# Attention and gated feed-forward on one core: the first slots' transposes, loads and copies put in another order

## The chip, the core and the metric

The kernel runs on one core of one Trainium2 chip. Its time is the device time of one execution in microseconds. Eleven runs gave a median of 563.99 us, the lowest 562.91 us and the highest 565.9 us. A run of the changed kernel is compared with runs of this one on the same chip.

## What is computed

Threshold attention over 8 batches of 8 heads, 576 positions, head size 64, then a two-layer block with a gated activation on the 4608 x 512 result:

```
scores = q @ k.T / sqrt(64)
scores = where(scores >= max(scores, row) - tau, scores, -1e9)
attn = softmax(scores)            # tau = 0.02
x = (attn @ v), heads side by side: 4608 x 512
h = x @ w_in                      # 512 -> 2048
g = h * clip(h + 3, 0, 6) / 6
out = g @ w_out                   # 2048 -> 512
```

Inputs and output are float32. The weights, the values and the normalised attention are kept on the chip in bf16, queries, keys and scores in float32.

## The kernel before

The 64 heads are taken in 16 quads of four heads. A quad is two pairs (pair 0 and pair 1 of the quad), and is worked off in nine **slots**: slots 0 to 3 are the four 128-row blocks of the first pair, 4 to 7 those of the second pair, and slot 8 holds the last 64 rows of all four heads. The 144 slots are numbered by n (the loop at L439); n = 9 x quad + slot. The order of the work on each engine is written out by hand: what the Python loop emits first stands first in its engine's queue, and each engine works in that order.

One turn of the loop does this, in order:
- ScalarE: the exponentials of the slot before (`sm_exp`, L291, two of 128 x 576).
- VectorE: the row maxima of this slot's scores, which also copy them out of PSUM (`sm_max`, L278, two), and on GpSimd the biases made from them (L281, two tiny ones).
- TensorE, from n = 23 on: a piece of the first layer (`mm1`, L354), its relu on ScalarE or VectorE (L363, L365) and its gate on VectorE (L371). All these use the one PSUM tile "h".
- TensorE: if slot n - 2 is marked `on_chip`, nine transposes of its normalised attention into the same tile "h" (L315), and a VectorE copy of them (L316). Slots not so marked are transposed by a DMA on SyncE's queue (L307). `on_chip` holds for odd n below N1 = 22.
- VectorE: the reciprocals of the row sums of slot n - 1 (L294). Then pieces of the second layer (`mm2_part`, L383).
- ScalarE: the masks of this slot (`sm_mask`, L286, two), which wait for the biases.
- TensorE: a transpose step for keys and queries (below), or the products of attention and values (`av_main`, `av_rest`, L324 and L327); then **the scores of the next slot** (L257 or L263), which need the next slot's queries and keys transposed and a free one of two score tiles.
- GpSimd: the normalisation of slot n - 1 (`sm_norm`, L299, two of 128 x 576), and SyncE's DMA transpose of it.
- The issue of loads: `start(loads, ...)` on SyncE's queue for q and k (L515), `start(vcasts, ...)` and `start(casts, ...)` on GpSimd's queue for v and the weights, which are cast to bf16 on the way (L516, L517). A GpSimd DMA stands in GpSimd's queue behind the normalisation and ahead of the next slot's biases.

The transpose step: the second pair's queries in slot 1 and keys in slot 2 of its own quad; the next quad's first pair in slots 5 and 6, and the rest rows of that quad in slot 7 (`transpose_rest`, L229). For the first two batches (quads 0 to 3) queries go through TensorE too. Each writes a PSUM bank, and is followed by copies to SBUF. Key copies go through `copy_out` (L200): VectorE while 0 <= n < 22, ScalarE before the loop and from n = 22 on. Query copies are always VectorE's. `transpose_rest` fills one bank with the keys' and the queries' rest and reads it with two key copies, and then one query copy.

Ahead of the loop: the q and k loads of quad 0 are issued in five steps (L154: first pair's keys, first pair's queries, the rest rows, second pair's keys, second pair's queries). TensorE transposes what the first slots need; GpSimd then makes a one-column copy of the transposed keys into a tile `gate` that nobody reads (L426), and issues the four loads of v behind it (L427). Weights come as 32 loads, 16 of w_in and then 16 of w_out. At L515 to L517 two q/k loads are started in each of the first three slots and then one, no v loads in the first 13 slots, and two weight loads in each of the first four and then one.

Of the kernel before, what the change touches and what calls it, by code (L numbers as in the profile page):

```python
# [9 lines left out]
F32 = mybir.dt.float32  # L10
# [5 lines left out]
P = 128  # L16
# [5 lines left out]
def kernel(  # L22
# [10 lines left out]
    nc = tc.nc  # L33
    B, H, S, D = q.shape
# [8 lines left out]
    N1 = 22  # L43
# [4 lines left out]
    singles = ctx.enter_context(tc.tile_pool(name="singles", bufs=1))  # L48
# [25 lines left out]
    loads = []  # L74
    casts = []
    vcasts = []
# [3 lines left out]
    def load_quad(quad):  # L80
        b, g = divmod(quad, 2)
        nat[quad] = (nat_pool.tile([P, 1152], F32, tag="nq", name="nq"),
                     nat_pool.tile([P, 4, 4, D], F32, tag="km", name="km"),
                     nat_pool.tile([P, 2 * D], F32, tag="kr", name="kr"))
        nq, km, kr = nat[quad]

        def main(dst, src, h, order):
            nc.sync.dma_start(out=dst[:, :, h, :], in_=src[b, 4 * g + h, 0:512, :].rearrange(order, t=4))

        def blocks_q(n, a, j):  # L90
            c = 32 * (2 * a + j)
            nc.sync.dma_start(out=nq[c:c + 32, n * S:(n + 1) * S].rearrange("p (k d) -> p k d", d=32),  # L92
                              in_=q[b, 4 * g + 2 * n + a, :, 32 * j:32 * j + 32].rearrange("(k r) d -> r k d", r=32))

        def load_q(n):
            if b < NB:
                for a in range(2):
                    main(nq[:, 0:1024].rearrange("p (t h d) -> p t h d", h=4, t=4), q, 2 * n + a, "(t p) d -> p t d")
            else:
                for a in range(2):  # L100
                    for j in range(2):
                        blocks_q(n, a, j)

        def rest():
            for dst, src in ((kr[:], k), (nq[:, 1024:1152], q))[0:2 if b < NB else 1]:
                for n in range(2):
                    nc.sync.dma_start(out=dst[64 * n:64 * n + 64, :].rearrange("p (h d) -> p h d", h=2),
                                      in_=src[b, 4 * g + 2 * n:4 * g + 2 * n + 2, 512:S, :].rearrange("h p d -> p h d"))

        for n in range(2):  # L110
            loads.append(lambda n=n: [main(km, k, 2 * n + a, "(p t) d -> p t d") for a in range(2)])
            loads.append(lambda n=n: load_q(n))
            if n == 0:
                loads.append(rest)
# [34 lines left out]
    def start(jobs, n):  # L149
        for _ in range(min(n, len(jobs))):  # L150
            jobs.pop(0)()
# [27 lines left out]
    def alloc_qk(quad):  # L179
        qkT[quad] = (qk_pool.tile([P, 2, S], F32, tag="qT", name="qT"),  # L180
                     qk_pool.tile([P, 2, S + 64], F32, tag="kT", name="kT"))
# [4 lines left out]
    def kT_of(pair):  # L186
        return qkT[pair // 2][1][:, pair % 2, :]
# [4 lines left out]
    def bank(name):  # L192
        nonlocal turn
        turn += 1
        if now < N2 and turn % 2:
            return ps_o.tile([P, 512], F32, tag="o", name=name)
        return ps_m.tile([P, 512], F32, tag="m", name=name)


    def copy_out(out, in_):  # L200
        if 0 <= now < N1:
            nc.vector.tensor_copy(out=out, in_=in_)
        else:
            nc.scalar.copy(out=out, in_=in_)  # L204


    def by_pe(pair):
        return pair // NPAIR < NB
# [16 lines left out]
    def transpose_k(pair):  # L225
        ps = main_pe(nat[pair // 2][1], pair)
        return lambda: copy_out(kT_of(pair)[:, 64:576], ps[:])

    def transpose_rest(quad):  # L229
        ps = bank("tr")  # L230
        nq, _, kr = nat[quad]
        nc.tensor.transpose(ps[:, 0:P], kr[:], identf[:])
        if by_pe(2 * quad):
            nc.tensor.transpose(ps[:, P:2 * P], nq[:, 1024:1152], identf[:])

        def evict():
            qT, kT = qkT[quad]
            both = ps[:].rearrange("p (w n t) -> p w n t", n=2, t=64)
            copy_out(kT[0:64, :, S:S + 64], both[0:64, 0])
            copy_out(kT[64:P, :, 0:64], both[64:P, 0])  # L240
            if by_pe(2 * quad):
                nc.vector.tensor_copy(out=qT[:, :, 512:S], in_=both[:, 1])
        return evict

    def keys(pair, a, hf):
# [43 lines left out]
    def sm_exp(sl, i):  # L289
        s = sl.s[:, i, :]  # L290
        nc.scalar.activation(out=s, in_=s, func=Act.Exp, accum_out=sl.rsum[:, i:i + 1])  # L291

    def sm_recip(sl):
        nc.vector.reciprocal(out=sl.rinv[:], in_=sl.rsum[:])  # L294
# [73 lines left out]
    def mm1_gate(item, hps, r):  # L368
        b, ni, c0, w = item
        c0 += (b % 2) * S  # L370
        nc.vector.scalar_tensor_tensor(out=gbuf[:, ni:ni + 2, c0:c0 + w], in0=r, scalar=6.0, in1=hps,  # L371
                                       op0=Alu.min, op1=Alu.mult)
# [42 lines left out]
        return items  # L415

    alloc_qk(0)
    gate = singles.tile([P, 1], F32)
    evict = transpose_k(0)
    warm_up(4)  # L420
    evict_q = transpose_q(0)
# [1 line left out]
    evict_q()  # L423
    transpose_rest(0)()

    nc.gpsimd.tensor_copy(out=gate[:], in_=kT_of(0)[:, 64:65])  # L426
    start(vcasts, 4)  # L427

    queue = []
    for quad in range(NQUAD):  # L430
        for slot in range(NSLOT):
            sl = Slot()
            sl.quad, sl.slot = quad, slot
            sl.on_chip = len(queue) < N1 and len(queue) % 2 == 1
            queue.append(sl)
    queue[0].tiles = scores(0, 0)

# [1 line left out]
    for n, sl in enumerate(queue):  # L439
        quad, slot = sl.quad, sl.slot  # L440
        b, g = divmod(quad, 2)
        now = n
        if slot in (0, 4):
            pts[2 * quad + slot // 4] = pt_pool.tile([P, 9, 512], BF16, tag="pT", name="pT")
        if slot == 8:
            ptr[quad] = ptr_pool.tile([P, 9, P], BF16, tag="pR", name="pR")
        if quad == 0 and slot == 0:
            load_quad(1)
        if slot == (4 if quad else 8) and quad + 2 < NQUAD:
            load_quad(quad + 2)  # L450
        if slot == 0 and g == 1 and b + 1 < B:
            load_v(b + 1)
        if prev is not None:
            for i in range(2):
                sm_exp(prev, i)
        sm_max(sl)

        if slot != 8 and todo1:
            item, then = todo1.pop(0)
            h = mm1(item)  # L460
            r = mm1_relu(h, on_act=(slot in (0, 1, 3, 5)))
            mm1_gate(item, h, r)
            todo2.extend(then)
        copies = pe_transpose(queue[n - 2]) if n > 1 and queue[n - 2].on_chip else None
        if prev is not None:
            sm_recip(prev)
        if copies:
            copies()
        outs = []


        pieces = 0 if slot == 3 else 1
        if slot == 0:
            second = True
        if second and slot < 2 and len(todo2) > 1 and todo2[0][1] == todo2[1][1]:
            pieces, second = 2, False
        for _ in range(pieces):
            if todo2:
                bb, mt, part = todo2.pop(0)
                mm2_part(bb, mt, part)  # L480
                if part == 3:
                    outs += mm2_out(bb, mt, on_act=False)
        for i in range(2):
            sm_mask(sl, i)
        evict = None
        nxt = 2 * quad + 2
        if slot == 1:
            evict = transpose_q(2 * quad + 1)
        elif slot == 2:
            evict = transpose_k(2 * quad + 1)  # L490
        elif slot == 3 and quad > 0:
            av_main(2 * quad - 1)
        elif slot == 4 and quad > 0:
            av_rest(quad - 1)
            if quad % 2 == 0:
                todo1.extend(moe_of(quad // 2 - 1))
        elif slot in (5, 6, 7) and quad + 1 < NQUAD:
            if slot == 5:
                alloc_qk(quad + 1)
                evict = transpose_q(nxt)  # L500
            elif slot == 6:
                evict = transpose_k(nxt)
            else:
                evict = transpose_rest(quad + 1)
        elif slot == 8:
            av_main(2 * quad)
        if evict:
            evict()
        if n + 1 < len(queue):
            queue[n + 1].tiles = scores(queue[n + 1].quad, queue[n + 1].slot)  # L510
        if prev is not None:
            sm_norm(prev)
        flush()
        late.extend(outs)
        start(loads, 2 if n < 3 else 1)  # L515
        start(vcasts, 1 if n > 12 else 0)  # L516
        start(casts, 2 if n < 4 else 1)  # L517
        prev = sl

    for i in range(2):  # L520
# [66 lines left out]
```

## Time and profile before

| | |
|---|---|
| median of 11 runs | 563.99 us |
| the profiled execution | 564.55 us, of which its span (first to last instruction) is 562.8 us |
| mean granted TensorE clock | 0.989 |
| quads 0, 1, 2 (start of the first row maximum to the next quad's) | 30.35, 27.51, 29.43 us |
| quads 3, 4, 5 | 32.60, 32.76, 32.06 us |
| quads 6 to 14 | 30.12 to 32.32 us each |

Busy times in the profile are per engine. "PEld" is TensorE's loading of weights, which runs beside its matmuls. In a timeline row the first number is the start in us from the span's beginning, the second the length from the first to the last of the merged instructions, and the bracket at the end tells how long the engine had stood idle before and what released it. A row of the table by windows gives the stretch, its length, the busy time (and count) of each engine, then the granted TensorE clock (1.00 is full), the mean load of the DMA engines, and GB/s.

### The profile page before, as it was taken

How to read it: one execution, taken by the hardware profiler on the slowest of the kernel's cores; microseconds unless marked ns; L12 is line 12 of the kernel's file. 1: busy time of each engine (PE TensorE's matmuls, PEld its weight loads, DVE VectorE, ACT ScalarE, POOL GpSimd, SP SyncE). 2: the span in 40 equal slices, each digit the busy share in tenths (PEclk: the TensorE clock that was granted, in tenths of full speed). 3: DMA queues.
4: the chain of work that ended last, by engine and by line, in shares of the span. 5: the costliest groups of instructions: out<-in, count | busy, mean ns of one | idle time of the engine just before them, and what ended most of it. 6: DMA issues, size and time to landing. Idle time of an engine off the chain costs nothing.

```text
span 562.8 us, 11556 instructions
## 1 busy us (share of the span) xinstructions
PE 530.8 (94%) x3817; PEld 305.1 (54%) x3817; DVE 425.4 (76%) x1041; ACT 469.4 (83%) x999; POOL 305.5 (54%) x647
## 2 busy tenths in 40 slices
PE   6798778999999999999999999999999999999996
PEld 4455345655545555555555565555555565654653
DVE  3578777797878888787878798887878798883540
ACT  4689897988988999989898999889898999983540
POOL 4678876654556556655456655655556555561000
PEclk9889999999999999999999999999999999999999
DMA  8979998967589877987589878987789965653102
GB/s 133 171 115 161 195 150 135 156 128 159 119 153 145 146 160 145 184 134 164 107 151 175 155 144 130 202 146 148 122 140 174 157 136 119 99 105 90 38 20 75
DMA packets 285020, 77.22 MB, mean 137 GB/s; under 512 B 268064, under 2 KB 280352, under 8 KB 284960
## 3 DMA queue, kind: packets, MB, share of 16 engines
q1 hardware_dynamic: 267552, 67.57, 65.7%
q0 software_dynamic: 17408, 8.92, 13.6%
q8 instruction: 30, 0.49, 0.4%
q14 instruction: 30, 0.25, 0.1%
HBM read 36.70 MB, written 9.44 MB: 82 GB/s over the span
## 4 chain that ended last, share of the span: by engine, by line
PE 58%; DVE 12%; ACT 8%; issue 3%; DMA 2%; SPq 2%; POOL 1%; DVEq 0%
PE o L383 17%; PE h L354 17%; PE s L257 15%; DVE s L278 6%; PE av L324 3%; ACT s L286 3%; DVE g L371 3%; ACT s L291 2%; DMA nq<-in_q_dram 2%; DVE r L365 2%; ACT r L363 2%; PE s L263 1%; PE tp L214 1%; SPq L92 1%; SPq L307 1%
## 5 line engine op out<-in xcount | busy, mean ns | idle before, releaser
L299 POOL TENSOR_SCALAR pn<-s,rinv 128x576 bf16<-128x576 f32 x288 | 211.6, 745 | 136.1 <-DVE rinv L294 63.2
L286 ACT ACTIVATE s<-s,bias 128x576 f32<-128x576 f32 x288 | 206.9, 766 | 38.1 <-POOL bias L281 36.8
L278 DVE TENSOR_SCALAR_CACHE_REDUCE s<-s 128x576 f32<-128x576 f32 x288 | 205.9, 752 | 40.5 <-PE s L257 30.9
L291 ACT ACTIVATE s<-s 128x576 f32<-128x576 f32 x288 | 192.7, 671 | 0.3
L257 PE MATMUL s<-kT,qT 64*128 64x288 f32 x1024 | 173.3, 436 | 5.9 <-DVE s L278 5.6
L354 PE MATMUL h<-xT,w_in_sb 128*128 128x320 bf16 (+1 forms) x1024 | 145.8, 288 | 4.6 <-DVE g L371 3.5
L383 PE MATMUL o<-w_out_sb,g 128*128 128x512 bf16 x576 | 140.9, 379 | 3.3 <-DVE osb L391 2.7
L257 PEld LDWEIGHTS s<-kT,qT 64*128 64x128 f32 x1024 | 95.6, 189 | 63.2 <-DVE s L278 27.6
L354 PEld LDWEIGHTS <-w_in_sb 128*128 128x128 bf16 x1024 | 92.3, 98 | 68.0 <-issue 30.3
L371 DVE SCALAR_TENSOR_TENSOR g<-r,h 128x512 bf16<-128x512 f32 (+1 forms) x128 | 96.4, 754 | 39.6 <-ACT r L363 37.6
L281 POOL TENSOR_SCALAR bias<-m 128x1 f32<-128x1 f32 x288 | 54.4, 189 | 61.9 <-DVE s L278 41.9
L383 PEld LDWEIGHTS <-g 128*128 128x128 bf16 x576 | 55.6, 98 | 57.9 <-issue 9.5
L363 ACT ACTIVATE r<-h,three 128x640 f32<-128x640 f32 (+1 forms) x74 | 54.4, 737 | 21.3 <-PE h L354 20.7
L291 ACT ACTIVATION_READ_ACCUMULATOR s<-s 128x1 f32 x288 | 54.2, 188 | 0.0
L365 DVE TENSOR_SCALAR r<-h 128x512 f32<-128x512 f32 (+1 forms) x54 | 40.5, 751 | 0.0
L391 DVE TENSOR_SCALAR osb<-o 128x512 f32<-128x512 f32 x31 | 21.0, 677 | 22.2 <-PE o L383 22.2
L324 PE MATMUL av<-pT,vm 128*64 128x512 bf16 x256 | 33.7, 385 | 0.4 <-ACT kT L204 0.4
L294 DVE RECIPROCAL rinv<-rsum 128x2 f32<-128x2 f32 x144 | 23.0, 160 | 11.2 <-ACT s L291 10.1
L324 PEld LDWEIGHTS <-vm 128*64 128x64 bf16 x512 | 17.8, 110 | 23.6 <-issue 16.6
L336 DVE CAST xT<-av 128x512 bf16<-128x512 f32 x32 | 21.8, 680 | 4.8 <-PE av L327 4.5
L278 DVE DVE_READ_ACCUMULATOR s<-s 128x1 f32 x288 | 23.9, 83 | 0.0
L389 ACT ACTIVATE osb<-o 128x512 f32<-128x512 f32 x5 | 3.0, 597 | 23.9 <-PE o L383 23.9
(43 smaller groups left out, 245.9 us busy)
## 6 DMA issues: line engine op xcount, KB each, us to landing
km<-in_k_dram SPq DMA_DIRECT2D x64, 128.0 KB, 3.1
out_dram<-osb SPq DMA_DIRECT2D x32, 256.0 KB, 2.5
nq<-in_q_dram SPq DMA_DIRECT2D x96, 72.0 KB, 2.8
vm<-in_v_dram POOLq DMA_DIRECT2D x16, 256.0 KB, 5.6
nq<-in_q_dram SPq DMA_DIRECT2D x16, 128.0 KB, 4.6
w_in_sb<-in_moe_w_in_dram POOLq DMA_DIRECT2D x16, 128.0 KB, 4.3
w_out_sb<-in_moe_w_out_dram POOLq DMA_DIRECT2D x16, 128.0 KB, 3.8
pT<-pn SPq DMA_TRANSPOSE x118, 3.4
```

The costliest lines, as they stand in the source:

```text
L257: nc.tensor.matmul(tiles[a][:, hf, 0:HALF], qT_of(pair)[a * 64:(a + 1) * 64, t * P:(t + 1) * P], keys(pair, a, hf), start=True, stop=True)
L278: nc.vector.tensor_scalar(out=sl.s[:, i, :].rearrange("p (a b) -> p a b", a=2), in0=ps[:, :, 0:HALF], scalar1=1.0, scalar2=None, op0=Alu.m ...
L281: nc.gpsimd.tensor_scalar(out=sl.bias[:, i:i + 1], in0=sl.m[:, i:i + 1], scalar1=-scale, scalar2=tau, op0=Alu.mult, op1=Alu.add)
L286: nc.scalar.activation(out=s, in_=s, func=Act.Prelu, bias=sl.bias[:, i:i + 1], scale=scale, alpha=REJECT)
L291: nc.scalar.activation(out=s, in_=s, func=Act.Exp, accum_out=sl.rsum[:, i:i + 1])
L299: nc.gpsimd.tensor_scalar(out=pn[:, i, :], in0=sl.s[:, i, :], scalar1=sl.rinv[:, i:i + 1], scalar2=1.0, op0=Alu.mult, op1=Alu.mult)
L324: nc.tensor.matmul(ps[a * 64:(a + 1) * 64, :], vm[:, 2 * hp + a, c * D:(c + 1) * D], pT[:, 5 * a + c, cols], start=(c == 0), stop=False)
L354: nc.tensor.matmul(hps[:, n, 0:w], w_in_sb[:, ki, (ni + n) * P:(ni + n + 1) * P], xT[b][:, ki, c0:c0 + w], start=(ki == 0), stop=(ki == KI ...
L363: nc.scalar.activation(out=r, in_=hps, func=Act.Relu, bias=three[:])
L365: nc.vector.tensor_scalar(out=r, in0=hps, scalar1=3.0, scalar2=0.0, op0=Alu.add, op1=Alu.max)
L371: nc.vector.scalar_tensor_tensor(out=gbuf[:, ni:ni + 2, c0:c0 + w], in0=r, scalar=6.0, in1=hps, op0=Alu.min, op1=Alu.mult)
L383: nc.tensor.matmul(o_ps[0], gbuf[:, ni, mt * P:(mt + 1) * P], w_out_sb[:, ni, :], start=(ni == 0), stop=(ni == NI - 1))
```

## The change

```diff
@@ transpose_rest
         def evict():
             qT, kT = qkT[quad]
             both = ps[:].rearrange("p (w n t) -> p w n t", n=2, t=64)
+            if by_pe(2 * quad):
+                nc.vector.tensor_copy(out=qT[:, :, 512:S], in_=both[:, 1])
             copy_out(kT[0:64, :, S:S + 64], both[0:64, 0])
             copy_out(kT[64:P, :, 0:64], both[64:P, 0])
-            if by_pe(2 * quad):
-                nc.vector.tensor_copy(out=qT[:, :, 512:S], in_=both[:, 1])
@@ ahead of the loop
-    gate = singles.tile([P, 1], F32)
...
-    nc.gpsimd.tensor_copy(out=gate[:], in_=kT_of(0)[:, 64:65])
-    start(vcasts, 4)
...
-            sl.on_chip = len(queue) < N1 and len(queue) % 2 == 1
+            sl.on_chip = len(queue) < N1 - 1 and len(queue) % 2 == 1
@@ in the loop
-        if slot == 1:
+        if slot == (1 if quad else 2):
             evict = transpose_q(2 * quad + 1)
-        elif slot == 2:
+        elif slot == (2 if quad else 3):
             evict = transpose_k(2 * quad + 1)
...
-        start(loads, 2 if n < 3 else 1)
-        start(vcasts, 1 if n > 12 else 0)
-        start(casts, 2 if n < 4 else 1)
+        start(loads, 1)
+        if n < 4 or n > 12:
+            start(vcasts, 1)
+        if n > 3:
+            start(casts, 1 if n < 24 else 2)
```

Six edits: (1) the query copy of `transpose_rest` stands ahead of the two key copies; (2) the `gate` copy is gone, and the four v loads of batch 0 are started one a slot in n = 0 to 3 instead of ahead of the loop; (3) slot 21 is no longer transposed on TensorE at n = 23, but by a DMA issued at n = 22; (4) in quad 0 alone the second pair's queries are transposed in slot 2 and its keys in slot 3; (5) q/k loads one a slot from the outset, so that quad 1's are issued in n = 0 to 4 instead of 0 to 2; (6) weight loads none in n = 0 to 3, one a slot in n = 4 to 23, two a slot from n = 24 until the 32 are out, which is n = 29 (before, the last was issued in n = 27).

## The prediction

> **What bounds the kernel now.** First the table by windows, in stretches of 20 and 40 us: it shows which engine is full where.
>
> ```profile
> 0.00:20.00 20.00, 13.97 (x64) 9.17 (x66) 7.15 (x22) 8.46 (x17) 8.59 (x23) 0.91 0.94 154
> 20.00:40.00 20.00, 16.78 (x111) 9.36 (x110) 14.74 (x41) 17.50 (x39) 16.23 (x35) 0.91 0.81 119
> ...
> 80.00:100.00 20.00, 16.55 (x115) 10.44 (x116) 13.91 (x38) 16.50 (x36) 12.00 (x26) 0.92 0.91 142
> ...
> 160.00:200.00 40.00, 39.03 (x279) 22.03 (x277) 30.97 (x76) 35.78 (x77) 23.00 (x48) 1.00 0.91 155
> ```
>
> From 160 us on TensorE (first number after the length) is busy 39 us of 40, at full clock: nothing there is touched, and what the start gains is passed on whole. Up to about 112 us no engine is full, and the clock dips in three stretches; all six edits lie there. The fullest engine is ScalarE (fourth number), so I follow its mask (L286), once in each slot. The list of waits gives ScalarE 8.0 us of idleness ahead of masks between 8 and 40 us, all put down to the bias. The timeline says what stands behind the bias:
>
> ```profile
> 14.95 1.09 PE L214 MATMUL tp<-identf,nq 128*128 128x128 f32 x4 [2.94 <-DMA nq<-in_q_dram]
> ...
> 19.37 1.45 ACT L286 ACTIVATE s<-s,bias 128x576 f32<-128x576 f32 x2 [3.57 <-POOL bias L281]
> ```
>
> At n = 1 TensorE stands 2.94 us before the second pair's query transposes, waiting for their load, with the scores of slot 2 queued behind; slot 2's mask starts 3.57 us late. Two later places have the same form, in quads 2 and 3:
>
> ```profile
> 84.28 0.66 PE L315 MATMUL pt<-identb,pn 128*128 128x128 bf16 x9 [1.64 <-DVE g L371]
> ...
> 87.75 1.45 ACT L286 ACTIVATE s<-s,bias 128x576 f32<-128x576 f32 x2 [1.59 <-POOL bias L281]
> ```
>
> At n = 23 slot 21's transposes need the tile "h" that the first `mm1` holds until its gate is through: 1.64 us, and the next mask is 1.59 us late.
>
> ```profile
> 93.89 0.29 DVE L242 COPY qT<-tr 128x128 f32<-128x128 f32 x1 [1.64 <-ACT kT L204]
> ...
> 94.91 2.07 PE L257 MATMUL s<-kT,qT 64*128 64x288 f32 x8 [1.61 <-DVE s L278]
> ...
> 102.79 0.54 POOL L146 DMA_DIRECT2D w_out_sb<-in_moe_w_out_dram  x1
> ...
> 103.62 1.44 ACT L286 ACTIVATE s<-s,bias 128x576 f32<-128x576 f32 x2 [0.86 <-POOL bias L281]
> ```
>
> At n = 25 VectorE's query copy waits 1.64 us for ScalarE's key copies, holds the row maximum of n = 26 up, and TensorE stands for 1.61 us. The last two rows: a weight load on GpSimd of 0.54 us stands ahead of slot 28's bias, and its mask is 0.86 us late.
>
> **Quad 0: edits 2, 4, 5 and the weights of the first slots.** Mask starts before, n = 1 to 8: 13.04, 19.37, 22.94, 26.11, 28.79, 32.62, 35.64, 38.32. I walk the slots again with the trace's durations: row maximum 1.44 for two, mask 1.45 for two, exponentials 1.34, normalisation 1.47, scores 1.31 to 1.91, 1.35 from scores to the first maximum, transposes 0.66 (fp32) and 0.85 (bf16), copies 0.68 and 0.74, GpSimd's v loads 0.80 and 0.65, weight load 0.58.
> - n = 0: the rest's query copy (0.29) now goes ahead of ScalarE's key copies, for which the first scores wait: +0.3, mask of n = 1 at 13.4.
> - n = 1: no transposes; scores(2) follow scores(1) at 12.6, maximum(2) 14.2 to 15.6. GpSimd normalises slot 0 until 15.2 and issues one v load until 16.05; the bias follows, mask(2) at 16.25: 3.1 earlier.
> - n = 2: query transposes behind scores(3); the load is long there. Mask(3) at 19.0, when ScalarE and the bias are both ready.
> - n = 3: here the edit **adds a wait**. The key transposes stand behind slot 1's nine transposes; the copy stands on VectorE behind reciprocal and pT copy (19.05 to 19.95) and ends at 20.6; scores(4) need it at once, where before a slot lay between. Queued behind: scores(4), maximum(4) at 22.0, bias and mask(4) at 23.0. ScalarE stands 1.2; the lead is 3.1 (26.11 before).
> - n = 5: before, slot 6's mask stood 1.07 us behind scores at half clock (below: the mask's row, then rows by windows whose number after TensorE to GpSimd is the clock, 0.50 at 29 and at 97, and TensorE's gap at 94). With one load instead of two on GpSimd and full clock I reach mask(6) at 28.95, mask(8) at 34.5: leads of 3.7 and 3.8.
>
> ```profile
> 32.62 1.45 ACT L286 ACTIVATE s<-s,bias 128x576 f32<-128x576 f32 x2 [1.07 <-POOL bias L281]
> ...
> 29.00:30.00 1.00, 1.00 (x5) 0.73 (x6) 1.00 (x3) 1.00 (x2) 0.75 (x2) 0.50 1.30 252
> ...
> 94.00:95.00 1.00, 0.09 (x1) 0.09 (x1) 1.00 (x4) 1.00 (x3) 0.45 (x2) 1.00 1.22 265
> ...
> 97.00:98.00 1.00, 1.00 (x6) 0.67 (x7) 1.00 (x4) 0.99 (x4) 0.92 (x3) 0.50 1.34 276
> ```
>
> The Trainium skill ("TensorE: Matmul & The Clock Gate", section "What's actually happening") has the clock halved after an idle window of about 3.4 us. By that rule the new stand of some 1.5 us at n = 3 costs no clock. The rows speak otherwise: a gap of 1.61 us, with TensorE working before and after it, was followed by half clock at 97. So at n = 3 the half clock may come too: a slot's scores then take 2.29 instead of 1.31. By the rule quad 0 yields 3.8, by the rows 2.8 if all of it reaches a mask; mask(5) has some slack behind its bias. I take **3.3**, ends 2.4 and 3.9.
>
> Beside that, at nothing: the `gate` copy (0.18) and the v loads, not needed before n = 8; quad 1's loads, one to two slots later on SyncE and behind slots 0's and 2's DMA transposes, needed from n = 5, issued from n = 0 (the last in n = 4, needed in n = 11; if that cover went, a slot would stall as n = 1 did, 3 us).
>
> **Slot 21: edit 3.** Gone: 1.64 of standing and 0.66 of transposes on TensorE, 0.76 of copy on VectorE. Next in line is the gate of n = 23 (84.23), then reciprocal, query copy, maximum(24) at 85.0 instead of 86.67. But GpSimd normalises until 86.03 and issues a load until 86.55, so mask(24) starts at 86.8, not 87.75: **1.0**. What is added: one DMA transpose on SyncE (1.3 to issue, 3.4 to land), ahead of a key load issued at 80.01 that is needed ten slots later: nothing, nor less than nothing.
>
> **The bank's copies: edit 1.** In quads 0 and 1 all three are VectorE's, so no time at n = 7 and 16. At n = 25 VectorE no longer waits: maximum(26) 1.4 earlier, TensorE's gap nearly closed, and the half clock of 97 to 100 gone (`mm1` 1.05 instead of 1.89). ScalarE is busy from 92.0 to 97.9 without a gap, so only the relu of n = 27, 0.85 late in that trace, can move: **0.9**.
>
> **Weights two a slot: edit 6's end.** Added on GpSimd: one in each of n = 24 to 27, two in n = 28 and 29, eight of 0.577 us, 4.6 us, each ahead of a bias for which a mask, and then the relu, wait. The skill's "DMA: Bandwidth & Descriptors" ("Issuing engines are not separate DMA queues") calls an issue's time usually small beside the transfer: 0.58 against 4.3 to landing agrees, and by that the cost is nothing. The row of 103.40 to 103.62 above says that such an issue sits on the path. Walking n = 24 to 30 with it, the leads of edits 3 and 1 over the trace at the mask are 1.05 (n = 25), 1.0 (26), 1.15 (28), 0.1 (29), 0 (30): GpSimd's loads at n = 28 and 29 (v 0.80 or 0.65, and 1.15 of weights) eat nearly all of it. Cost: between 0 and 4.6; I take **1.6**, so that edits 1, 3 and 6 together give 0.3 of 1.9.
>
> **Sum.** 3.3 + 1.0 + 0.9 - 1.6 = 3.6. Against the profiled execution: span 562.8 - 3.6 = 559.2, and with the 1.75 around it 560.95. That execution is 0.56 above the median, so 563.99 - 3.6 = **560.4**. The program of PE-bound quads behind is the same and should repeat.
>
> **The rivals.**
> - *The loads on GpSimd are hidden* (one is late only where two were before): then 3.6 + 1.9 = 5.2 from quad 0 at 3.3 plus both later gains: 558.8. For it: GpSimd idles a third of 80 to 112. Against: it idles waiting for reciprocals, and the load comes after that wait. Chance 0.20.
> - *The new wait at n = 3 takes most of the gain*: half clock from 21 on, and a late bias; quad 0 gives 1.0 or less, the rest nothing: 563.0 to 563.9. For it: the gap is of the size that halved the clock at 97; against: TensorE has no other wait in these slots. Chance 0.12.
> - *Slower: GpSimd's queue at n = 24 to 29*. All 4.6 on the path, the leads of edits 1 and 3 not realised since masks wait for biases anyhow, quad 0 at 2.4: 563.99 + 4.6 - 2.4 = 566.2. It decides from the point at which these loads cost more than quad 0 yields. Against: at n = 26 ScalarE is full and a late bias costs nothing. Chance 0.08.
> - *Main case*, 560.4, chance 0.60.
>
> **How the numbers follow.** A measurement of this kernel can tell about 0.2%, 1.1 us, from no change. The main case (558.9 to 562.2) and the first rival are faster: 0.80. The second gives same, 0.12; the third slower, 0.08. The range leaves out the slower rival and most of the second: 558.0 to 562.7.
>
> **What would show it.** Right: no wait for nq before L214 in quad 0; mask(2) at about 16.2; quad 0 from 30.35 to some 27; one stand of ScalarE at n = 4 of about 1.2; "PE pt <- DVE g" gone; maximum(26) right behind maximum(25)'s work; masks of n = 28 to 30 behind GpSimd's loads; later quads as long as before. Wrong: a second pair's load still late, half clock through quad 0, or quad 3 longer than 32.6 by more than quad 2 became shorter.

## The result, and the profile after

The changed kernel took 562.2 us (median of 13 runs, 561.36 to 565.36); the kernel before took 565.27 us (48 runs, 562.26 to 567.54) beside it. The ratio is 0.9951, 95% interval 0.9936 to 0.9967: faster by 0.5%, some 2.8 us. A second comparison on another occasion gave 0.9953 (0.9937 to 0.9969). The profiled execution has a span of 559.6 us, 3.2 under that of before, in a run of 561.36 us.

Below, **lead** is how much earlier a slot's first row maximum (L278) starts than in the profile of before, **mask lead** the same for the slot's first mask (L286), and **half clock** a granted TensorE clock of 0.50. From both timelines, in us:

| slot n | 2 | 3 | 4 | 6 | 8 | 18 | 22 | 24 | 26 | 28 | 29 | 31 | 36 | 72 | 135 |
|---|---|---|---|---|---|---|---|---|---|---|---|---|---|---|---|
| lead | 3.40 | 1.50 | 0.09 | 2.73 | 2.82 | 2.81 | 2.81 | 4.67 | 6.43 | 5.48 | 4.41 | 3.36 | 3.35 | 3.34 | 2.98 |

Three stages can be told apart: quad 0 brings 2.8; slots 22 to 36 bring another 0.54, after a peak that is mostly given back; behind slot 36 the programs run alike, 0.35 being lost in one step at n = 124, which the second profile of the changed kernel shows too. The timeline of the changed kernel in quad 0 (start, length, and in brackets the idle time before and its releaser):

```profile
15.73 1.11 PE L214 MATMUL tp<-identf,nq 128*128 128x128 f32 x4
...
16.38 1.44 ACT L286 ACTIVATE s<-s,bias 128x576 f32<-128x576 f32 x2
...
20.18 1.45 ACT L286 ACTIVATE s<-s,bias 128x576 f32<-128x576 f32 x2 [1.03 <-POOL bias L281]
...
21.19 0.68 DVE L202 COPY kT<-tp 128x512 f32<-128x512 f32 x1
...
21.92 1.24 PE L257 MATMUL s<-kT,qT 64*128 64x288 f32 x8 [1.28 <-DVE kT L202]
...
24.36 1.45 ACT L286 ACTIVATE s<-s,bias 128x576 f32<-128x576 f32 x2 [1.40 <-POOL bias L281]
```

The wait of 2.94 us for the queries' load is gone: the transposes, now in slot 2, start at 15.73 without a bracket. Slot 2's mask starts at 16.38, 19.37 before. Slot 3's mask (20.18) is late by 1.03, which is half clock, and slot 4's (24.36) by 1.40: that is the new wait, the scores of slot 4 standing 1.28 us behind the key copy on VectorE. The clock, by windows (after the five engines' busy times; 1.00 is full):

```profile
10.00:11.00 1.00, 0.61 (x3) 0.29 (x2) 1.00 (x3) 0.21 (x1) 0.19 (x1) 1.00 0.95 217
...
11.00:12.00 1.00, 1.00 (x7) 0.68 (x6) 0.15 (x2) 1.00 (x2) 0.70 (x2) 1.00 0.28 63
...
12.00:13.00 1.00, 0.61 (x3) 0.17 (x2) 0.99 (x3) 1.00 (x4) 0.55 (x2) 1.00 0.00 0
...
13.00:14.00 1.00, 1.00 (x4) 0.61 (x6) 0.62 (x3) 1.00 (x3) 0.38 (x3) 0.65 0.78 98
...
16.00:17.00 1.00, 1.00 (x6) 0.67 (x7) 0.80 (x4) 0.86 (x3) 0.47 (x4) 0.50 0.11 11
...
19.00:20.00 1.00, 1.00 (x12) 1.00 (x11) 0.91 (x3) 0.15 (x2) 0.08 (x2) 0.50 1.31 200
```

TensorE was busy 61% or more of each microsecond from 10 to 13, and still fell to half clock at about 13.3, for some 6.8 us. The second profile of the changed kernel has the same three shares (0.61, 1.00, 0.61) and stayed at full clock there.

Slots 24 to 29, again from the timeline:

```profile
84.04 1.44 ACT L286 ACTIVATE s<-s,bias 128x576 f32<-128x576 f32 x2 [0.68 <-POOL bias L281]
...
87.49 0.27 DVE L240 COPY qT<-tr 128x128 f32<-128x128 f32 x1
...
88.55 0.75 PE L257 MATMUL s<-kT,qT 64*128 64x288 f32 x2
...
89.20 0.51 ACT L204 COPY kT<-tr 64x128 f32<-64x128 f32 x2
...
97.02 0.80 POOL L121 DMA_DIRECT2D vm<-in_v_dram  x1
...
97.82 1.07 POOL L146 DMA_DIRECT2D w_out_sb<-in_moe_w_out_dram  x2
...
99.18 1.44 ACT L286 ACTIVATE s<-s,bias 128x576 f32<-128x576 f32 x2 [1.26 <-POOL bias L281]
...
101.73 1.08 POOL L146 DMA_DIRECT2D w_out_sb<-in_moe_w_out_dram  x2
...
103.10 1.44 ACT L286 ACTIVATE s<-s,bias 128x576 f32<-128x576 f32 x2 [1.15 <-POOL bias L281]
```

Slot 24's mask is at 84.04, 3.71 earlier than before. The query copy at 87.49 no longer waits, and TensorE's next scores stand 0.47 us in their midst for ScalarE's key copies, where they stood 1.61 us ahead of them before. At n = 27 and 28 the pair of weight loads (97.82, 101.73) stands behind a v load, and the masks of slots 28 and 29 are 1.26 and 1.15 us late behind it. The mask lead adds this up: 2.81 at slot 23, 3.71 at 24, 4.15 at 25, 4.97 at 27, then 4.44 at 28 and 3.36 at 29. So 2.16 us are won and 1.61 given back.

### The profile page after: what moved, and what is told of

Same layout as the page of the kernel before. It is cut to its first block, busy times and chain, and to the rows that moved or that the text cites. A ratio compares the mean times of both kernels' runs of the same rounds, so it can differ in the third digit from the quotient of the medians.

```text
span 559.6 us, 11539 instructions
## 1 busy us (share of the span) xinstructions
PE 530.9 (95%) x3808; PEld 305.7 (55%) x3808; DVE 424.2 (76%) x1040; ACT 469.7 (84%) x999; POOL 305.3 (55%) x646
## 4 chain that ended last, share of the span: by engine, by line
PE 61%; DVE 11%; ACT 6%; issue 2%; DMA 2%; SPq 2%; POOL 1%; DVEq 0%
PE h L354 18%; PE o L383 18%; PE s L257 17%; DVE s L278 5%; PE av L324 4%; DVE g L371 3%; ACT s L286 2%; ACT s L291 2%; DVE r L365 2%; DMA nq<-in_q_dram 2%; PE tp L214 1%; PE s L263 1%; ACT r L363 1%; PE av L327 1%; DVE osb L391 1%
## 5 line engine op out<-in xcount | busy, mean ns | idle before, releaser
L278 DVE TENSOR_SCALAR_CACHE_REDUCE s<-s 128x576 f32<-128x576 f32 x288 | 205.9, 752 | 42.3 <-PE s L257 31.9
L286 ACT ACTIVATE s<-s,bias 128x576 f32<-128x576 f32 x288 | 206.9, 766 | 35.0 <-POOL bias L281 33.8
L257 PEld LDWEIGHTS s<-kT,qT 64*128 64x128 f32 x1024 | 95.2, 188 | 65.3 <-DVE s L278 27.8
L278 DVE DVE_READ_ACCUMULATOR s<-s 128x1 f32 x288 | 24.0, 83 | 0.0
```

Source lines behind the costliest of these rows:

```text
L257: nc.tensor.matmul(tiles[a][:, hf, 0:HALF], qT_of(pair)[a * 64:(a + 1) * 64, t * P:(t + 1) * P], keys(pair, a, hf), start=True, stop=True)
L278: nc.vector.tensor_scalar(out=sl.s[:, i, :].rearrange("p (a b) -> p a b", a=2), in0=ps[:, :, 0:HALF], scalar1=1.0, scalar2=None, op0=Alu.m ...
L286: nc.scalar.activation(out=s, in_=s, func=Act.Prelu, bias=sl.bias[:, i:i + 1], scale=scale, alpha=REJECT)
```

## The experiments

Thirteen profiles, of the changed kernel and of variants of both kernels, are laid beside that of before. The table has, for each, the ratio of times to the kernel before run beside it with its interval, the time at half clock in the first 33 us (summed from windows of 1 us), and leads. The last column is the gain or loss of slots 22 to 36 alone.

| kernel | median us | ratio (95%) | half clock to 33 us | lead n = 8 | n = 22 | n = 36 | 22 to 36 |
|---|---|---|---|---|---|---|---|
| before | | | 6.8 | 0 | 0 | 0 | 0 |
| changed | 562.2 | 0.9951 (0.9936-0.9967) | 6.8 | 2.82 | 2.81 | 3.35 | +0.54 |
| changed, again | 562.8 | 0.9953 (0.9937-0.9969) | 3.4 | 2.74 | 2.74 | 3.27 | +0.53 |
| edits 1, 3 undone | 565.93 | 1.0013 (0.9993-1.0033) | 10.2 | 1.39 | 0.73 | -3.40 | -4.13 |
| edit 1 undone | 563.17 | 0.9953 (0.9935-0.9971) | 6.8 | 2.17 | 2.10 | 1.21 | -0.89 |
| weights single | 562.44 | 0.9929 (0.9903-0.9955) | 10.2 | 1.47 | 1.41 | 2.98 | +1.57 |
| edit 4 undone | 559.62 | 0.9894 (0.9858-0.9931) | 0 | 5.61 | 5.57 | 5.05 | -0.52 |
| edit 4 undone, again | 560.1 | 0.9894 (0.9875-0.9914) | 10.2 | 2.79 | 2.79 | 3.33 | +0.54 |
| edit 4 undone, weights single | 560.5 | 0.9902 (0.9868-0.9937) | 3.4 | 3.64 | 3.54 | 5.09 | +1.55 |
| both steps in slot 2 | 559.29 | 0.9885 (0.9865-0.9905) | 0 | 5.72 | 4.12 | 4.65 | +0.53 |
| edit 4 alone | 563.63 | 0.9958 (0.9941-0.9976) | 10.2 | 1.54 | 1.48 | 0.95 | -0.53 |
| v later alone | 563.07 | 0.9957 (0.9931-0.9983) | 0 | 5.08 | 2.27 | 3.05 | +0.78 |
| gate back | 563.16 | 0.9946 (0.9926-0.9966) | 6.8 | 2.85 | 1.15 | 1.65 | +0.50 |
| idle transposes at n = 1 | 562.23 | 0.9943 (0.9923-0.9963) | 13.6 | 0.31 | 0.30 | 0.83 | +0.53 |

Half clock comes in pieces of 3.4 us, and the same program has one, two or three of them in quad 0 from one execution to the next. So a lead in a single profile is read together with its half clock, and the medians over several runs decide what a version is worth. Later pieces count too: the 1.6 us that "both steps in slot 2" loses from n = 8 to 22 lie beside one at 64.9, the 1.7 of "gate back" beside one at 67.8.

**Edits 1 and 3 undone.** Theory: GpSimd's weight loads at n = 24 to 29 cost time, and edits 1 and 3 pay for them. Rival: what edits 1 and 3 win is lost again whatever GpSimd does.

```diff
-            if by_pe(2 * quad):
-                nc.vector.tensor_copy(out=qT[:, :, 512:S], in_=both[:, 1])
             copy_out(kT[0:64, :, S:S + 64], both[0:64, 0])
             copy_out(kT[64:P, :, 0:64], both[64:P, 0])
+            if by_pe(2 * quad):
+                nc.vector.tensor_copy(out=qT[:, :, 512:S], in_=both[:, 1])
...
-            sl.on_chip = len(queue) < N1 - 1 and len(queue) % 2 == 1
+            sl.on_chip = len(queue) < N1 and len(queue) % 2 == 1
```

> The changed kernel with the old order of the bank's copies and slot 21 on TensorE again; the outset, the v loads and the weights two a slot from n = 24 stay. Lead = how much earlier a slot's first row maximum starts than in the profile of before. My theory (GpSimd's loads at n = 24 to 29 cost, edits 1 and 3 pay for them): lead 2.8 us at n = 18 as in the changed kernel, then falling to 1.2 to 2.0 from n = 32 on; 562 to 563 in the profiled run. Rival (edits 1 and 3 bring nothing that lasts, because what they win is lost again whatever GpSimd does): lead stays at 2.8 to 3.4 to the end, as in the changed kernel.

Measured: no gain at all (1.0013), and slots 22 to 36 lose 4.13 us. The rival falls: this interval and that of the changed kernel don't overlap. The theory has the sign, but the loss is far above the 0.8 to 1.6 it gave. (0.64 of the lead had gone before, at n = 22, where the products with the values waited 0.56 us for a DMA transpose.) Its timeline:

```profile
90.40 1.12 POOL L146 DMA_DIRECT2D w_out_sb<-in_moe_w_out_dram  x2
...
91.81 1.44 ACT L286 ACTIVATE s<-s,bias 128x576 f32<-128x576 f32 x2 [1.52 <-POOL bias L281]
...
99.60 0.69 ACT L363 ACTIVATE r<-h,three 128x512 f32<-128x512 f32 x1 [1.80 <-PE h L354]
...
103.56 1.07 POOL L146 DMA_DIRECT2D w_out_sb<-in_moe_w_out_dram  x2
...
104.92 1.44 ACT L286 ACTIVATE s<-s,bias 128x576 f32<-128x576 f32 x2 [1.39 <-POOL bias L281]
...
107.47 1.08 POOL L146 DMA_DIRECT2D w_out_sb<-in_moe_w_out_dram  x2
...
108.84 1.44 ACT L286 ACTIVATE s<-s,bias 128x576 f32<-128x576 f32 x2 [1.15 <-POOL bias L281]
```

Each of these three pairs of weight loads (L146 x2, 1.1 us) is followed by a mask that comes 1.15 to 1.52 us late, those of slots 25, 28 and 29; the masks of slots 26 and 27 don't wait for theirs. This profile has also 6.8 us at half clock from 94.6 and 3.4 from 111.7, where the kernel before has 3.4 from 96.7 and the changed one 3.4 from 95.2. Slot by slot, the mask lead falls by 0.53, 0.54 and 1.08 at slots 25, 28 and 29, directly behind loads: 2.15. It falls by 0.95 at slot 27, where the relu ahead of the mask waits 1.80 us for TensorE, and by 1.0 in slots 32 and 35, both times behind half clock. So about half of the 4.13 are loads. "Edit 4 alone" and "v later alone", which have neither edit 1 nor 3 but one weight load a slot here, change by -0.53 and +0.78 over the same slots. This was also the slowest of its version's runs, 2.1 us above their median; by the medians edits 1 and 3 are worth some 3.5 us here.

**Weights single.** The same question from the other end.

```diff
-        if n > 3:
-            start(casts, 1 if n < 24 else 2)
+        if n != 1:
+            start(casts, 1)
```

> The changed kernel with one weight load in every slot but n = 1 until the 32 are out (n = 32), never two. My theory: quad 0 as in the changed kernel (lead about 2.8 at n = 18), the peak of 4.7 to 6.4 in n = 24 to 26 stays, and less of it is given back: lead 4.2 to 5.0 from n = 32 on, 1 to 1.6 us faster than the changed kernel. Rival (the lead of n = 26 is lost to half clock on TensorE at 95 to 99 us and to ScalarE being full, not to GpSimd): lead 3.0 to 3.5 from n = 32 on, as in the changed kernel. Second rival (weight loads in n = 0, 2 and 3 delay the first biases): lead at n = 18 falls to 2.2 or less.

Slots 22 to 36 bring 1.57 instead of 0.54, and with the transposes back in slots 1 and 2 they bring 1.55. So, with edits 1 and 3 in place, doubling the weight loads costs 1.0 us in the profiles. The lower lead in quad 0 (1.47) goes with a third piece of half clock in this profile, as in the other three-piece profiles with the shift (1.39, 1.54), so the second rival isn't needed, though its sign (2.2 or less at n = 18) did appear. The final lead is below the forecast because quad 0's was; in the medians the version is not to be told from the changed kernel (0.9929 against 0.9951, intervals overlap). Its timeline beside that above: one load, and a mask 0.61 us late where it was 1.15.

```profile
102.08 0.54 POOL L146 DMA_DIRECT2D w_out_sb<-in_moe_w_out_dram  x1
...
102.91 1.44 ACT L286 ACTIVATE s<-s,bias 128x576 f32<-128x576 f32 x2 [0.61 <-POOL bias L281]
```

The rival of that run, that the lead of n = 26 is lost to half clock at 95, falls by the second profile of the changed kernel: it has no half clock between 60 and 125 us and still goes from 6.34 at n = 26 to 3.28 at n = 32.

**Edit 1 undone.** Now the order of the bank's copies alone goes back, with the same lines as in the first experiment.

> The changed kernel with the old order of the bank's copies. By what the run without edits 1 and 3 showed (5 us lost from n = 22 to 32): n = 24 still gains 1.9 over n = 22, at n = 26 the gain shrinks to about 0.5 because VectorE waits for ScalarE, half clock follows at 95; change of lead from n = 22 to n = 32 between -3 and -1, against +0.5 in the changed kernel. If edit 1 matters as the prediction said (0.9): change -0.4.

```profile
88.58 1.44 ACT L286 ACTIVATE s<-s,bias 128x576 f32<-128x576 f32 x2 [0.56 <-POOL bias L281]
...
89.92 0.52 ACT L204 COPY kT<-tr 64x128 f32<-64x128 f32 x2
...
90.47 0.29 DVE L242 COPY qT<-tr 128x128 f32<-128x128 f32 x1 [2.18 <-ACT kT L204]
...
91.49 2.63 PE L257 MATMUL s<-kT,qT 64*128 64x288 f32 x8 [2.15 <-DVE s L278]
```

VectorE's query copy (L242 here) waits 2.18 us for ScalarE's two, which stand behind a mask; TensorE's scores wait 2.15. Slots 22 to 36 lose 0.89 instead of winning 0.54, which lies between the two forecasts. The difference of 1.4 stands in one place: at slot 27 the mask lead falls by 0.55, where the changed kernel's rises by 0.82. Half clock from 92.7 lies just ahead of it.

The gap alone costs the masks nothing: "v later alone", below, has the old order and the same gap (1.62 us), but no half clock behind it, and its mask lead rises by 0.82 at slot 27 too. Two of its rows, the gap and the relu of n = 27, which doesn't wait:

```profile
92.65 1.98 PE L257 MATMUL s<-kT,qT 64*128 64x288 f32 x8 [1.62 <-DVE s L278]
...
95.76 0.69 ACT L363 ACTIVATE r<-h,three 128x512 f32<-128x512 f32 x1
```

With the old order four of five profiles have half clock between 92 and 101 us, with the new one one of nine. So edit 1 seems to pay by making that piece rarer or harmless. The medians don't show it (0.9953 without it, 0.9951 and 0.9953 with it). Edit 3 was never undone alone, so how the pair's 3.5 us divides stays open.

**Edit 4 undone, edit 4 alone.** Which of edits 2, 4 and 5 made quad 0's gain?

```diff
-        if slot == (1 if quad else 2):
+        if slot == 1:
             evict = transpose_q(2 * quad + 1)
-        elif slot == (2 if quad else 3):
+        elif slot == 2:
             evict = transpose_k(2 * quad + 1)
```

> The changed kernel with the second pair's transposes of quad 0 back in slots 1 and 2. If the load of that pair's queries was late because the v loads ran beside it, it now comes in time (12 us or before), n = 1 has no wait, n = 3 has no new wait: lead at n = 18 about 3.5 to 4. If the load is late by itself, TensorE waits at n = 1 for 1 to 3 us and the lead at n = 18 is 0 to 2: then it is the shift by a slot that brought quad 0's gain.

> The kernel before with nothing but the second pair's transposes of quad 0 one slot later; gate, v loads ahead of the loop and two weight loads in the first slots stay. If the shift alone makes quad 0's gain: lead at n = 18 2 to 3. My theory is that it brings most of it: 1.5 to 2.5, the rest lost to GpSimd's two loads a slot ahead of the biases of n = 1 to 4; final lead the same as at n = 18. If the v loads' contention is the cause, it brings less than 1.

With the transposes back in slots 1 and 2 and all else as changed, the kernel is faster: 559.62 us, 0.9894. The lead, 5.6, is above both forecasts, in a profile without half clock in quad 0. Its timeline:

```profile
12.40 0.66 PE L214 MATMUL tp<-identf,nq 128*128 128x128 f32 x4
...
16.41 1.44 ACT L286 ACTIVATE s<-s,bias 128x576 f32<-128x576 f32 x2
...
19.11 1.44 ACT L286 ACTIVATE s<-s,bias 128x576 f32<-128x576 f32 x2
...
21.83 1.44 ACT L286 ACTIVATE s<-s,bias 128x576 f32<-128x576 f32 x2
```

The query transposes of n = 1 run at 12.40 without a wait, and the masks of slots 2, 3, 4 follow one another at 2.7 us with no idle time: the load is no longer late. The tile's view gives issue to landing of the second pair's query load (minimum, median and maximum of its two halves), first in the kernel before, then in this one:

```profile
DMA to landing us min/median/max: 6.6/6.7/6.8
```

```profile
DMA to landing us min/median/max: 2.8/2.9/3.0
```

The shift alone, in the kernel before, is faster than before too (0.9958), with a lead of 1.54 at n = 8. So the shift cures the wait as well, though here the load itself still lands late (5.2 to 6.9 us).

**v later alone, gate back.** The same from the side of edit 2: the v loads moved with everything else as before (weights two a slot in n = 4 to 11 to make room), and the changed kernel with the v loads ahead of the loop again.

```diff
# v later alone, in the kernel before (gate and start(vcasts, 4) taken out)
-        start(vcasts, 1 if n > 12 else 0)
-        start(casts, 2 if n < 4 else 1)
+        start(vcasts, 1 if n < 4 or n > 12 else 0)
+        start(casts, 0 if n < 4 else 2 if n < 12 else 1)
# gate back, in the changed kernel
+    nc.gpsimd.tensor_copy(out=gate[:], in_=kT_of(0)[:, 64:65])
+    start(vcasts, 4)
...
-        if n < 4 or n > 12:
+        if n > 12:
             start(vcasts, 1)
```

> The kernel before with the gate gone and the four v loads one a slot in n = 0 to 3, and to make room for them no weights there, two a slot in n = 4 to 11 and then one (the last in n = 27, as before). Transposes, copies and slot 21 as before. If edit 2 alone makes quad 0's gain: no wait for queries at n = 1, no half clock in quad 0, lead at n = 8 4 to 5.6, from which two weight loads a slot may take up to 1 by n = 12; final lead as at n = 18. Rival (the shift by a slot is needed): TensorE waits for queries at n = 1 as before, lead below 2.

> The changed kernel with the gate copy and the four v loads back ahead of the loop; the second pair's transposes stay one slot later, weights start at n = 4. Two theories of quad 0's gain. Moving v (edit 2) frees the load of the second pair's queries: then here that load lands late again, but with the transposes in slot 2 it is waited for less or not at all: lead at n = 18 about 1.4 to 2.8, as in the changed kernel, since edit 4 hides the lateness. If v's loads hurt beyond that load: lead below 1.

v later alone: the query load lands after 2.7 to 3.0 us, there is no wait at n = 1 and no half clock in quad 0, and the lead is 5.96 at n = 6 and 5.08 at n = 8. Its loads of q and k go as before, so edit 5, which no run tests alone, isn't needed for it. Then it falls to 2.33 by n = 12, much more than the "up to 1" that was expected. GpSimd is the reason that the timeline shows: each pair of weight loads makes the next mask about 0.40 us late. The masks of slots 5 to 11 follow one another at 3.17 us, all but the last of them ahead of the one piece of half clock, which begins at 41.8.

```profile
39.08 1.12 POOL L142 DMA_DIRECT2D w_in_sb<-in_moe_w_in_dram  x2
...
40.50 1.44 ACT L286 ACTIVATE s<-s,bias 128x576 f32<-128x576 f32 x2 [0.40 <-POOL bias L281]
...
42.25 1.12 POOL L142 DMA_DIRECT2D w_in_sb<-in_moe_w_in_dram  x2
...
43.67 1.44 ACT L286 ACTIVATE s<-s,bias 128x576 f32<-128x576 f32 x2 [0.40 <-POOL bias L281]
```

Gate back: that load lands late again (5.4 to 7.2 us; 3.0 to 3.1 in the changed kernel, which differs in nothing but the v loads and the `gate` copy). So it was the v loads that made it late. The view of the changed kernel, then of gate back:

```profile
DMA to landing us min/median/max: 3.0/3.1/3.1
```

```profile
DMA to landing us min/median/max: 5.4/6.3/7.2
```

In gate back nobody waits for that load in slot 2, the lead at n = 8 is 2.85, and the time is the changed kernel's (0.9946 and 0.9951). With edit 4 in the kernel, edit 2 brings nothing that can be measured: the two edits cure the same wait.

**Where edit 4 loses: both steps in slot 2, idle transposes at n = 1.** Two candidates: the wait at n = 3, and TensorE's lower load at n = 1, which might bring the half clock.

```diff
# both steps in slot 2
+        if quad == 0 and slot == 2:
+            evict_q1, evict_k1 = transpose_q(1), transpose_k(1)
+            evict = lambda: (evict_q1(), evict_k1())
# idle transposes at n = 1: results not read, nothing else altered
+        if n == 1:
+            idle = ps_m.tile([P, 512], F32, tag="m", name="idle")
+            for t in range(4):
+                nc.tensor.transpose(idle[:, t * P:(t + 1) * P], identf[:], identf[:])
```

> The changed kernel with the second pair's queries and keys both transposed in slot 2 of quad 0, so that n = 3 has no key copy for which the next scores wait. If the wait at n = 3 is the larger part of edit 4's cost: ScalarE's idle time before the mask of n = 4 falls from 1.4 to under 0.5, lead at n = 8 3.8 to 5. If the half clock is the larger part: the wait at n = 3 goes but half clock stays, lead at n = 8 2.8 to 3.6.

> The changed kernel with four added transposes of the identity at n = 1, into a bank that nobody reads, where the second pair's query transposes used to stand. They only keep TensorE busy. If the half clock from 13 us on (six to seven us long in all profiles with the shifted transposes) comes from TensorE doing too little at n = 1, it is gone or comes later, and the lead at n = 8 rises from 2.8 to 3.5 to 4.5; the wait of some 1.3 us at n = 3 stays. If the clock falls whatever stands at n = 1, or the wait at n = 3 is all that edit 4 costs: lead 1.4 to 2.8 as in the other runs with the shift.

Both steps in slot 2: 559.29 us, 0.9885 (0.9865 to 0.9905), the fastest version of the study, though not to be told from edit 4 undone. The wait at n = 3 is gone, and in this profile quad 0's half clock too, so the lead (5.72) lies above both forecasts. Three rows of quad 0's window, first the kernel before, then this one, then the second profile of the changed kernel (ScalarE is the fourth engine, the clock the number behind the five):

```profile
8.00:36.80 28.80, 22.15 (x127) 12.49 (x128) 17.75 (x50) 20.77 (x46) 19.56 (x43) 0.88 1.04 155
```

```profile
8.00:36.80 28.80, 24.92 (x162) 14.42 (x163) 22.21 (x64) 26.20 (x58) 21.82 (x47) 1.00 0.90 145
```

```profile
8.00:36.80 28.80, 23.59 (x142) 13.17 (x142) 20.00 (x56) 23.39 (x52) 19.09 (x41) 0.94 0.81 123
```

ScalarE does 26.20 us of work in that stretch, against 23.39 and 20.77. And the mask of slot 4 follows without a bracket, at 21.73:

```profile
19.00 1.44 ACT L286 ACTIVATE s<-s,bias 128x576 f32<-128x576 f32 x2
...
21.73 1.44 ACT L286 ACTIVATE s<-s,bias 128x576 f32<-128x576 f32 x2
```

The idle transposes tell nothing of what they were made for: in that profile half clock began at about 11.2, ahead of them, and came back at 24.8 (13.6 us in all, lead 0.31). The median (0.9943) is that of the changed kernel. That TensorE's load at n = 1 decides the clock is not shown.

**The changed kernel and edit 4 undone, on one chip.**

> The changed kernel with the second pair's transposes of quad 0 in slots 1 and 2, once more, beside the changed kernel itself on one chip: 559.5 to 561, 1.5 to 3 us under the changed kernel's median; lead at n = 8 3.6 with one stretch of half clock in quad 0, 5.6 with none.

> The changed kernel itself, for comparison on the same chip: median 561.8 to 563, 0.4 to 0.6 per cent under the kernel before; lead at n = 8 1.4 with three stretches of half clock in quad 0, 2.8 with two.

560.1 against 562.8 us, 0.9894 (0.9875 to 0.9914) against 0.9953 (0.9937 to 0.9969): the intervals don't overlap. Undoing edit 4 is worth some 0.6%, 3 us, about as much again as the whole change brought. The two profiles don't show it (lead 2.79 and 2.74), since the one without the shift had three pieces of half clock, the changed kernel one. With half clock about equal the order is right: three pieces, 2.79 without the shift, 1.39 to 1.54 with it; one piece, 3.64 without, 2.74 with. The difference, 0.9 to 1.4, is about what the wait at n = 3 was seen to take.

The rest is clock. On this chip the mean granted clock was 0.9888 over the eight runs of the changed kernel, 0.9953 over the six with edit 4 undone and 0.9970 over the four with both steps in slot 2. The times of the first two differ by 3.08 us in the mean. At 2.5 us for each 0.01 of clock (the line through the eight runs, last section), 1.6 of it is clock by estimate, and some 1.4 is left for the wait. "Both steps in slot 2" leaves n = 1 as empty as the changed kernel does and has the highest clock: this speaks for the step at n = 3 as what brings the half clock, and against the emptier n = 1, but four runs don't prove it.

The wait at n = 3 in the second profile of the changed kernel, and a later wait at half clock:

```profile
22.99 1.45 ACT L286 ACTIVATE s<-s,bias 128x576 f32<-128x576 f32 x2 [1.25 <-POOL bias L281]
...
30.14 1.45 ACT L286 ACTIVATE s<-s,bias 128x576 f32<-128x576 f32 x2 [1.34 <-POOL bias L281]
```

**Edit 4 undone, weights single.** Do the two findings add up?

> The changed kernel with two things altered: the second pair's transposes back in slots 1 and 2, and one weight load a slot, never two. If both findings add up: lead 5.6 at n = 18 and about 1.5 more from n = 32 on, 7.1, so about 7 us faster than before and 1 to 2 us faster than the run with only the transposes back. If the slots 24 to 32 are bound by something else once the start is earlier (half clock): lead 5.0 to 5.6 at the end.

Not as forecast. The 1.55 from n = 22 to 36 is there again, but on a lead of 3.54, with one piece of half clock in quad 0 where the run it builds on had none: 5.09 in the end, not 7.1. In the medians the single loads bring nothing on top of edit 4 undone (560.5, 0.9902).

## Why the prediction was right, and which step was not

It gave 560.4 us, a gain of 3.6, from a median of 563.99. Measured were 0.9951, a gain of 2.8 against runs that had a median of 565.27, and 3.2 between the two spans. The main case happened, with the size of each stage near the forecast:

- **Quad 0, 3.3 (2.4 to 3.9)**: 2.82 and 2.74 at n = 8 in two profiles. The walk's masks, 16.25 and 19.0 for slots 2 and 3, were 16.38 and 20.18 in the first profile (half clock), 16.28 and 18.97 in the second. That the two leads agree is in part chance: the first lost to half clock from 13.3 on and kept slot 6 free, the second the other way round.
- **The new wait at n = 3, ScalarE standing 1.2**: 1.40 and 1.25. That half clock may come behind such a gap was weighed; in the second profile it came at 25.4, and slot 6's mask was 1.34 late.
- **Slot 21, 1.0 at mask(24)**: 0.90, and 0.44 more at slot 25.
- **The bank's copies, 0.9 at the relu of n = 27**: 0.82 at slot 27's mask.
- **Weights two a slot, 1.6**: 1.61 at the masks of slots 28 and 29, and 1.0 by taking the doubling away. The three together, forecast 0.3: 0.54.

Two slips in the prediction's text cost nothing. The first rival's "3.6 + 1.9 = 5.2" should read 3.3 + 1.9. And in slot 2 the query transposes stand ahead of scores(3) on TensorE, not behind them (15.73 and 16.77 in the first profile).

**The step that failed is the account of quad 0.** The prediction put the v loads among the things "at nothing" and gave the gain to n = 1 having no transposes. In fact moving the v loads, with no weights in the first four slots, frees the query load (2.9 us to landing instead of 6.7), takes the wait away and gives a lead of 5 to 6 in a profile without half clock. The shift alone gives 1.5 in one with three pieces of it. In the medians each alone is worth about what all six edits are together (0.9957 and 0.9958, against 0.9951): with both, the shift hides what edit 2 does and adds the wait at n = 3. The number came out right because the walk started from what both edits together leave. The walk had its answer in hand: it has "the load is long there" at n = 2, and didn't ask whether it was there at n = 1.

**The slower rival** was in part a real mechanism: where edits 1 and 3 are missing, the kernel is no faster than before. But the loads took 2.15 us of the masks' lead there, not the 4.6 of its upper bound, and quad 0's lead in that profile was 1.39, not 2.4. The prediction's costs aren't independent: edits 1 and 3 are worth 4.7 us in the profiles in company with edit 6 (+0.54 against -4.13), and some 3.5 by the medians, not the 1.9 that was added up; the clock is in both.

Open: what decides in which of the 3.4 us pieces TensorE gets half clock, what edit 3 is worth alone, and whether edit 1 brings anything where no half clock comes.

## What to carry to other kernels

When a change moves both the waiter and what made the thing waited for late, walk each of them alone: two cures of one wait don't add, and the one left over may still have its price. A queue that issues loads ahead of a small operation on the path (here the bias on GpSimd) makes each load's issue time count, unless another engine is full just then, as ScalarE was at slot 26. And where executions of one program differ by whole pieces of half clock, compare one profile with another only beside their clocks, and let the medians decide.

## What the runs showed of the hardware

- Half clock came in pieces of 3.4 us or multiples (3.4, 6.8), 0 to 13.6 us in the first 33 us, and differently in executions of one program: the changed kernel at 13.3 to 20.1 once, at 25.4 to 28.8 the other time. Eight runs of the changed kernel on one chip lie close to a line of 2.5 us for each 0.01 of mean clock (correlation -0.99). In its thirteen runs of the first comparison the tie is looser (-0.71): the slowest, 565.36 us, had the same 0.988 as one of 562.2. So the clock is a large part of the spread, not all of it.
- It doesn't take an idle stretch of that length: with TensorE busy 61% to 100% of each microsecond, it fell at 13.3, and in another execution with the same shares it didn't. A gap of 1.61 us was followed by half clock in the kernel before, one of 1.62 in "v later alone" was not. The rule that the prediction cited from the Trainium skill ("TensorE: Matmul & The Clock Gate", "What's actually happening": an idle window of about 3.4 us) asks for more than these traces show.
- Four v loads (ahead of the loop) beside the plain loads of 128 KB each took their landing from 3.0 to 3.1 us to 5.4 to 7.2 (the changed kernel without and with the v loads ahead of the loop).
- A pair of weight loads takes 1.1 us of GpSimd's queue. The masks that waited behind such pairs were 0.40 to 1.52 us late; those of slots 26 and 27, in the profile without edits 1 and 3, didn't wait for theirs.
